# Gated linear attention with an ELU layer on one core: states of both halves in the first small group, values two slots later in one group with the next sums of logarithms, seam transfers on the sync queue

## The chip, the cores and the metric

The kernel runs on one core of a Trainium2 chip. The metric is the device time in microseconds of one execution. The engines are named as in the profile: PE is TensorE's matmul side and PEld its weight load, DVE is VectorE, ACT is ScalarE, POOL is GpSimd, SP is SyncE, which here only issues DMAs. Each engine takes its instructions in the order in which they stand in its queue; between engines, semaphores order what depends on each other.

## The reference

Two parts. The first is a gated recurrence over 768 positions, for 4 sequences and 8 heads of dimension 48, with a complex decay per position, head and row. The second is a two-layer network with an ELU over the 3072 x 384 outputs of the first (weights 384 x 2048 and 2048 x 384).

```python
mag = np.sqrt(a_re * a_re + a_im * a_im)
scale = np.minimum(mag, 0.999) / (mag + 1e-06)
...
for t in range(S):
    ar, ai = (a_re_n[:, :, t, :, None], a_im_n[:, :, t, :, None])
    new_re = ar * S_re - ai * S_im
    new_im = ar * S_im + ai * S_re
    kv = np.einsum('bhd,bhe->bhde', k[:, :, t], v[:, :, t])
    S_re, S_im = (new_re + kv, new_im)
    y[:, :, t] = np.einsum('bhd,bhde->bhe', q[:, :, t], S_re)
...
h = x @ w_in
g = np.where(h > 0.0, h, np.exp(np.minimum(h, 0.0)) - 1.0)
return g @ w_out
```

All data are float32 (the weights come as float64 and are rounded on the chip).

## The kernel before

The work is cut into twelve groups `u` = 0 to 11 (`NU`), each of two sequences (`NB`, here called the two halves `n`) times 128 positions (`C`), and each half into two chunks of 64 positions (`L`, index `c`). Groups 4 and up (`PAIRED`) are all done in the same way, and the change concerns these.

For one group the recurrence goes as follows. The decays become logarithms and angles: `squares` (L709, L710 on ACT), `joined` (L716 on POOL), `logarithms` (L735, L736), `powers` (L746, L747), `lengths` (L772 on DVE; its result is `l`), `ratios` (L759, L760 on POOL), `slopes` (L780 on DVE), `angles` (L815 on ACT) and `carried` (L821 on DVE). `decays` sums the logarithms along the positions: `quartered` makes four matmuls of 64x64 weights and 384 columns (L883) into two `w` buffers, and six exponentials on ACT (L893) turn them into the scales `E` and `F`; a DMA on ACT's queue stores the last rows of `E`, from which `ends` fetches the chunk decays `T`. `turns` sums the angles (L832 on PE), `waves` takes sine and cosine, `scaled` and `gated` apply them to the keys and queries, `transposed` (L1008) turns those.

Then come the small groups of matmuls. `scored` makes the products of keys and values of the first half (`state_products(u, 0)`, L1048, two `w` buffers), the scores of both halves (L1118, into the buffer `y`), the new states of the first half (`state_sums`: L1063 on DVE adds, L1065 on POOL multiplies with `T`) and the masked scores (L1125 on DVE). `valued` makes the products of the second half (L1048), the scores times the values of both halves (`value_products`, L1081), the states of the second half (L1063, L1065), the old states times the queries (`carried_products`, L1090, sorted by chunk), and copies the result to `x` and `y` in SBUF (L1144, L1145 on ACT). `seam` moves the rows of the last pairs of heads from `y` to their places in `x`: six DMAs of 16 KB (L1157), issued by POOL from group 2 on.

The layer of a group follows its attention: eight times `inner` (twelve recorded matmuls of 256 columns each, L1177, into a `mlp` buffer) with `elu` (L1186 and L1187 on ACT, L1188 on DVE), and `folded` (L1261 on DVE). The second product is made as seven products `k` on combined blocks, each in two parts `h` of four matmuls (eight records of 192 columns, L1283), in the order (1,0), (4,0), (1,1), (4,1), (6,0), (6,1), (5,0), (5,1), (7,0), (7,1), (2,0), (2,1), (3,0), (3,1). Products 1, 2 and 6 share one `mlp` buffer, one PSUM bank: 1 and 2 fill its first half of columns, 6 its second. After (1,1) ACT copies the first half to SBUF (L1291), and after (6,1) DVE adds the second half to that copy (L1295). Results go out through `o` buffers (L1302 on ACT, L1304 on DVE) by DMAs of the sync queue (L1305).

The order of all this is a table written by hand. `put(at, fn, ...)` gives each step a slot, the steps are sorted by slot, and each engine gets its instructions in that order (no scheduler changes it). A group has 16 slots; with `r = (u - 2) * 16`, the layer of group `u - 1` is multiplied out in slots r + 28 to r + 36 while group `u` is in `valued` and group `u + 1` is prepared. In these slots stood, in order: product (1,0), `logarithms` and `powers` of the next group (r + 28), (4,0), (1,1), `valued` and `seam` (r + 29.3), `lengths` and `ratios` of the next, (4,1), (6,0), (6,1), `slopes`, `decays` of the next (r + 31), (5,0) and so on; `turns` of the next at r + 34; the `inner` steps that read `x` begin at r + 36. `test_fetch` (L665, L670) loads pieces of the weights on the sync queue for a check by DVE (L680).

PSUM has three `w` buffers, three `mlp` buffers and one `y` of two banks.

Of the kernel before, what the change touches and what calls it, by code (L numbers as in the profile page):

```python
# [16 lines left out]
C = 128  # L17
# [488 lines left out]
def kernel(  # L506
# [13 lines left out]
    B, H, S, D = q.shape  # L520
    DM, DF = moe_w_in.shape[0], moe_w_out.shape[0]
    NI, NF = DM // C, DF // C
# [48 lines left out]
    def work(shape, tag="w"):  # L571
        return ps.tile(shape, FP32, tag=tag, bufs=3, name=tag)
# [120 lines left out]
    def new(tag, bufs=1, shape=None):  # L693
        return sb.tile(shape or [C, NB, H, D], FP32, tag=tag, bufs=bufs, name=tag)
# [182 lines left out]
    def quartered(u):  # L877

        x = nat[u]
        both = [work([C, HD]) for n in range(NB)]  # L880
        for c in range(C // L):
            for n, t in enumerate(both):
                nc.tensor.matmul(  # L883
                    t[ts(c ^ n, L)], lhsT=sum_logs[ts(c, L), ts(c, L)],
                    rhs=flat(x["l"][ts(c, L), n : n + 1]), start=True, stop=True,
                )
        for n, t in enumerate(both):
            for key, sign in (("E", 1.0), ("F", -1.0)):
                pairs = [(slice(0, C), slice(0, C))]
                if n:  # L890
                    pairs = [(ts(c, L), ts(1 - c, L)) for c in range(C // L)]
                for to, of in pairs:
                    nc.scalar.activation(  # L893
                        out=flat(x[key][to, n : n + 1]), in_=t[of], func=AF.Exp, scale=sign
                    )
        ends = dram.tile([NB, C // L, H, D], FP32, tag="ends", bufs=2, name="ends")
        nc.scalar.dma_start(
            out=ends.rearrange("n c h d -> c n (h d)"),
            in_=x["E"][L - 1 :: L].rearrange("p n h d -> p n (h d)"),
        )  # L900
        x["ends"] = ends
# [11 lines left out]
    def decays(u):  # L913
        x = nat[u]
        if u > 1:
            x["E"], x["F"] = new("n", 6), new("n", 6)
            quartered(u)
            return
        for n in range(NB):
            x["sums", n] = work([C, HD])  # L920
            nc.tensor.matmul(
                x["sums", n], lhsT=sum_logs, rhs=x["l"][:, n].rearrange("p h d -> p (h d)"),
                start=True, stop=True,
            )
            decayed(u, n)
# [103 lines left out]
    def state_products(u, n):  # L1029

        x = nat[u]
        b, s = where(u)
        x["S", n] = [state.get(b + n)]
        if s == S - C:
            last = C // L - 1
        else:
            last = C // L
        x["G", n] = gs = [
            work([C, H, D], "w" if u else "mlp") for c in range(last)
        ]  # L1040
        for h in range(H):
            for c, g in enumerate(gs):
                k = gates["k"][ts(c, L), n, h]
                parts = [(g[ts(i, HP), h], k[:, i]) for i in range(2)]
                if u == 0:
                    parts = [(g[:, h], k.rearrange("p i d -> p (i d)"))]
                for to, of in parts:
                    nc.tensor.matmul(  # L1048
                        to, lhsT=of, rhs=vn[u % 2][ts(c, L), n, ts(h, D)], start=True, stop=True,
                    )  # L1050

    def state_sums(u, n, chunks=range(C // L)):
        x = nat[u]
        for c, g in list(enumerate(x["G", n])):
            if c not in chunks:
                continue
            old = x["S", n][-1]
            new_s = new("S", 8, [C, H, D])
            wide = x["T"][:, n, c].unsqueeze(2).to_broadcast([C, H, D])
            if old is None:  # L1060
                nc.vector.tensor_tensor(out=new_s, in0=g, in1=wide, op=ALU.mult)
            else:
                nc.vector.tensor_tensor(out=new_s, in0=g, in1=old, op=ALU.add)  # L1063
                eng = nc.vector if u < 2 else nc.gpsimd
                eng.tensor_tensor(out=new_s, in0=new_s, in1=wide, op=ALU.mult)  # L1065
            x["S", n].append(new_s)
        state[where(u)[0] + n] = x["S", n][-1]
# [17 lines left out]
            )  # L1085
    def carried_products(u, n, y):
        x = nat[u]
        for p, c, j in EACH if u < PAIRED else sorted(EACH, key=lambda x: x[1]):
            if x["S", n][c] is not None:
                nc.tensor.matmul(  # L1090
                    y[ds(j * HP, D), c, ts(p, L)], lhsT=x["S", n][c][:, 2 * p + j],
                    rhs=x["qt", n][:, 2 * p + j, ts(c, L)], start=False, stop=False,
                    skip_group_check=True,
                )
# [15 lines left out]
    def scored(u):  # L1110

        x = nat[u]
        state_products(u, 0)
        t = ps.tile([C, NB, 512], FP32, tag="y", bufs=1, name="y")
        for n in range(NB):
            for h in range(H):
                for c in range(C // L):
                    nc.tensor.matmul(  # L1118
                        t[ts(c, L), n, ts(h, L)], lhsT=x["kt", n][:, h, ts(c, L)],
                        rhs=x["qt", n][:, h, ts(c, L)], start=True, stop=True,  # L1120
                    )
        for n in range(NB):
            state_sums(u, 0, [n])
            x["a", n] = new("a", 2, [C, H, L])
            nc.vector.tensor_tensor(  # L1125
                out=x["a", n], in0=t[:, n].rearrange("p (h t) -> p h t", h=H),
                in1=mask.unsqueeze(1).to_broadcast([C, H, L]), op=ALU.mult,
            )

    def valued(u):  # L1130

        x = nat[u]
        y = ps.tile([C, C // L, 512], FP32, tag="y", bufs=1, name="y")
        state_products(u, 1)
        for n in range(NB):
            value_products(u, n, y[:, :, ts(n, NP * L)], n == 0)
        state_sums(u, 1)
        for n in range(NB):
            carried_products(u, n, y[:, :, ts(n, NP * L)])
        x["x"], x["y"] = new("x", 2, [C, NI, GT]), new("y", 1, [C, GT])  # L1140
        parts = y.rearrange("p c (n x t) -> p c n x t", n=NB, x=NP)
        to = x["x"].rearrange("p x (n c t) -> p c n x t", n=NB, c=C // L)
        for c in range(C // L):
            nc.scalar.copy(out=to[:, c], in_=parts[:, c, :, 0:NI])  # L1144
        nc.scalar.copy(  # L1145
            out=x["y"].rearrange("p (n c t) -> p c n t", n=NB, c=C // L), in_=parts[:, :, :, NI],
        )

    def seam(u):

        x = nat[u]
        for j in range(2):
            for i in range(NI):
                eng = nc.scalar if u < 2 and j else nc.gpsimd
                if u == 0 and i == NI - 1:
                    eng = nc.sync
                eng.dma_start(  # L1157
                    out=x["x"][ds(j * HP + D, G), i], in_=x["y"][ds(j * HP + i * G, G)]
                )
# [232 lines left out]
    def put(at, fn, *args):  # L1392
        if fn is hidden:
            plan.append((at, len(plan), inner, args))
            plan.append((at, len(plan), elu, args))
        else:
            plan.append((at, len(plan), fn, args))
# [8 lines left out]

    def gates_of(u, *at):
        for x, fn in zip(at, (decays, turns, waves, scaled, ends, gated)):
            put(x, fn, u)

    def values_of(u, *at):
        fns = (transposed, "q"), (transposed, "k"), (scores,), (states,), (values,)
# [77 lines left out]
    for u in range(2, NU):  # L1490
        r = (u - 2) * SLOTS
        put(r + 8, load_a, u)
        put(r + 8, load_v, u)
        put(r + 8, load_qk, u)
        if u == 2:
            decays_of(u, 16, 17, 17, 18.4, 19.5, 19.6, 22.7, 19.8, 19.8)
            gates_of(u, 20.4, 21.6, 22.1, 22.4, 22.4, 22.6)
        else:
            decays_of(u, r + 11, r + 12, r + 12, r + 13.4, r + 13.5, r + 14.9, r + 16.7, r + 15.5, r + 16.6)
            gates_of(u, r + 15, r + 18, r + 18.5, r + 18, r + 18, r + 19.5)  # L1500
        if u < PAIRED:
            values_of(u, *(max(r + 22, 24.5) + x for x in (0, 1, 2, 3, 5, 4, 5, 6, 7, 8, 9)))
        else:
            for n in range(NB):
                put(r + 22 + 2 * n, transposed, u, "q", n)
                put(r + 23 + 2.3 * n, transposed, u, "k", n)
            put(r + 26.6, scored, u)
            put(r + 29.3, valued, u)
            put(r + 29.3, seam, u)
        layer_of(u, range(r + 36, r + 44), range(r + 44, r + 52))  # L1510
    for m in range(NR):
        put(40 + 4 * m, test_fetch, m)
# [42 lines left out]
```

## Time and profile before

| What | Value |
|---|---|
| Median of three runs | 698.71 us (697.7 to 698.75) |
| Profiled execution, whole | 700.76 us |
| Its span, first to last instruction | 699.0 us |
| Mean granted TensorE clock | 0.991 |
| Groups 4 to 11: start of `scored` (first L1048) | 249.00, 302.27, 355.70, 408.97, 462.25, 515.51, 570.23, 624.95 us |
| L1065 on POOL, mean | 936 ns |
| L1048 on PE, 1280 records of 64x64 | 25.8 us busy |
| L1157 on POOL's queue, 65 issues | 31.9 us busy, landing after 1.6 us (median) |

The profile's lines name engine, source line, operation and tiles; a float32 matmul leaves two records. In the timeline the columns are start, length, engine, line, operation, tiles, and the number of instructions merged; a bracket holds the idle time ahead and what ended it. Matmuls are pipelined and their ends are modelled, so lengths on PE are best read as the distance from one start to the next. A list of waits gives the total, the number of times and the longest.

### The profile page before, as it was taken

To read this page: it belongs to the slowest core of one execution; us is meant where nothing else is said; L and a number is where in the kernel's file an instruction comes from. 1 tells how busy PE (TensorE), PEld (TensorE's weight loads), DVE (VectorE), ACT (ScalarE), POOL (GpSimd) and SP (SyncE) were. 2 spreads that over 40 slices of the span, in tenths; PEclk is the share of its full clock that TensorE was granted. 3 is DMA by queue.
4 is the path that set the end of the run, shared out by engine and by line. 5 is a ranking of instruction groups with operands and counts; after the bars stand their busy time and mean duration, and the time that the engine had idled before them with its cause. 6 is when DMAs were issued, how large, how long until landed. Compare 5 with 4: busy or idle time off the path is not lost.

```text
span 699.0 us, 15744 instructions
## 1 busy us (share of the span) xinstructions
PE 665.2 (95%) x6656; PEld 580.0 (83%) x6656; DVE 399.6 (57%) x579; ACT 397.5 (57%) x622; POOL 201.6 (29%) x207
## 2 busy tenths in 40 slices
PE   8899899998999999999999999999999999999996
PEld 6777786565788898898998998998998888889995
DVE  5889999814857554555555555555555644742151
ACT  6875445658556754755755655656656547551230
POOL 2000000125423425425425415415408305402000
PEclk9899999999999999999999999999999999999999
DMA  9995746062082902911911821931831731200000
GB/s 163 174 160 94 156 150 173 10 115 53 3 137 67 144 26 63 141 31 59 142 37 53 131 52 53 131 55 51 118 67 30 143 63 31 69 1 8 23 1 28
DMA packets 149899, 55.98 MB, mean 80 GB/s; under 512 B 129172, under 2 KB 142652, under 8 KB 149820
## 3 DMA queue, kind: packets, MB, share of 16 engines
q1 hardware_dynamic: 146240, 53.53, 40.7%
q0 software_dynamic: 3360, 1.22, 1.3%
q8 instruction: 54, 0.88, 0.6%
q14 instruction: 25, 0.20, 0.1%
q10 hardware_dynamic: 220, 0.14, 0.1%
HBM read 48.88 MB, written 4.78 MB: 77 GB/s over the span
## 4 chain that ended last, share of the span: by engine, by line
PE 72%; DVE 11%; ACT 7%; POOL 5%; issue 3%; DMA 1%; ACTq 1%; POOLq 0%; DVEq 0%
PE mlp L1177 32%; PE mlp L1283 19%; PE w L1008 6%; DVE g L1261 3%; PE y L1118 2%; PE w L1048 2%; PE mlp L1198 2%; PE w L832 2%; PE y L1090 2%; DVE n L780 1%; DVE g L1188 1%; POOL S L1065 1%; PE w L1016 1%; DVE wf L43 1%; PE mlp L1386 1%
## 5 line engine op out<-in xcount | busy, mean ns | idle before, releaser
L1177 PE MATMUL mlp<-x,w_in 128*128 128x256 f32 x1152 | 262.3, 382 | 2.9 <-DVE g L1188 2.4
L1177 PEld LDWEIGHTS mlp<-x,w_in 128*128 128x128 f32 x1152 | 215.8, 191 | 32.5 <-DVE g L1188 2.8
L1188 DVE SCALAR_TENSOR_TENSOR g<-ee,mlp 128x512 f32<-128x512 f32 x96 | 65.5, 685 | 125.4 <-ACT ee L1187 119.2
L1186 ACT ACTIVATE ee<-mlp 128x512 f32<-128x512 f32 x96 | 57.3, 597 | 133.6 <-PE mlp L1177 125.4
L1283 PE MATMUL mlp<-w_out,g 128*128 128x192 f32 x640 | 110.3, 326 | 0.0
L1283 PEld LDWEIGHTS mlp<-w_out,g 128*128 128x128 f32 x640 | 105.4, 190 | 2.7
L1065 POOL TENSOR_TENSOR S<-S,T 128x384 f32<-128x384 f32 x36 | 33.7, 936 | 192.0 <-DVE S L1063 192.0
L1261 DVE TENSOR_TENSOR g<-g 128x512 f32<-128x512 f32 x80 | 67.3, 842 | 2.7
L1187 ACT ACTIVATE ee<-ee 128x512 f32<-128x512 f32 x96 | 60.5, 631 | 2.9
L1283 PEld LDWEIGHTS mlp<-w,g 128*128 128x128 f32 x320 | 52.0, 190 | 5.1 <-issue 4.8
L1283 PE MATMUL mlp<-w,g 128*128 128x192 f32 x320 | 56.0, 329 | 0.0
L856 POOL DMA_DIRECT2D carry<-n x10 | 5.3, 525 | 137.4 <-DVE n L840 137.4
L988 POOL TENSOR_TENSOR kg<-k,cs 128x1536 f32<-128x1536 f32 x9 | 38.6, 4294 | 19.8 <-issue 19.7
L1157 POOL DMA_DIRECT2D x<-y x65 | 31.9, 497 | 43.2 <-ACT y L1105 37.1
L893 ACT ACTIVATE n<-w 64x384 f32<-64x384 f32 (+1 forms) x60 | 28.1, 486 | 27.8 <-PE w L883 27.1
L1302 ACT COPY o<-mlp 128x192 f32<-128x192 f32 x10 | 3.2, 319 | 63.7 <-DMA out_dram<-o 52.9
L780 DVE SCALAR_TENSOR_TENSOR n<-n 128x768 f32<-128x768 f32 x11 | 13.7, 1247 | 35.7 <-POOL n L760 35.7
L1198 PE MATMUL mlp<-w_out,g 128*128 128x384 f32 x96 | 32.9, 490 | 0.7 <-DVE g L1188 0.7
L1063 DVE TENSOR_TENSOR S<-w,S 128x384 f32<-128x384 f32 x38 | 21.0, 553 | 21.5 <-PE w L1048 11.7
L1009 ACT COPY qt<-w 128x512 f32<-128x512 f32 x48 | 25.6, 581 | 12.7 <-PE w L1008 12.7
L716 POOL TENSOR_TENSOR n<-n 128x768 f32<-128x768 f32 x9 | 19.8, 2197 | 40.1 <-ACT n L710 40.1
L1090 PE MATMUL y<-qt,S 128*48 128x64 f32 x704 | 25.0, 222 | 6.0 <-POOL S L1065 4.1
(173 smaller groups left out, 988.5 us busy)
## 6 DMA issues: line engine op xcount, KB each, us to landing
w<-in_moe_w_out_dram SPq DMA_DIRECT2D x8, 768.0 KB
g<-in_moe_w_in_dram SPq DMA_DIRECT2D x16, 384.0 KB
g<-in_moe_w_out_dram SPq DMA_DIRECT2D x16, 384.0 KB
w<-in_moe_w_in_dram SPq DMA_DIRECT2D x16, 288.0 KB
vn<-in_v_dram SPq DMA_DIRECT2D x24, 192.0 KB
out_dram<-o SPq DMA_DIRECT2D x48, 96.0 KB
ar<-in_a_re_dram SPq DMA_DIRECT2D x22, 192.0 KB
ai<-in_a_im_dram SPq DMA_DIRECT2D x22, 192.0 KB
```

What stands on the lines that cost most here:

```text
L988: eng.tensor_tensor(out=to[:, :, :, 0:D], in0=each.unsqueeze(2).to_broadcast([C, step * H, 2, D]), in1=x["cs"][:, n * H : (n + step) * H], ...
L1008: nc.tensor.transpose(t[:, h], of, ident)
L1065: eng.tensor_tensor(out=new_s, in0=new_s, in1=wide, op=ALU.mult)
L1090: nc.tensor.matmul(y[ds(j * HP, D), c, ts(p, L)], lhsT=x["S", n][c][:, 2 * p + j], rhs=x["qt", n][:, 2 * p + j, ts(c, L)], start=False, st ...
L1157: eng.dma_start(out=x["x"][ds(j * HP + D, G), i], in_=x["y"][ds(j * HP + i * G, G)])
L1177: nc.tensor.matmul(t[:, e], lhsT=w_in[:, i, ts(f + e, C)], rhs=x["x"][:, i], start=(i == 0), stop=(i == NI - 1),)
L1186: nc.scalar.activation(out=e, in_=t, func=AF.Relu, scale=-1.0)
L1187: nc.scalar.activation(out=e, in_=e, func=AF.Exp, scale=-1.0)
L1188: nc.vector.scalar_tensor_tensor(out=x["g", f // 8][:, f % 8 : f % 8 + 2], in0=e, scalar=-1.0, in1=t, op0=ALU.add, op1=ALU.max)
L1198: nc.tensor.matmul(x["o", n], lhsT=x["g", f // 8][:, f % 8, ts(n, C)], rhs=w_out[:, f], start=(f == 0), stop=(f == NF - 1),)
L1261: nc.vector.tensor_tensor(out=S_of(u, k, h), in0=a, in1=b, op=op)
L1283: nc.tensor.matmul(to, lhsT=a[:, m], rhs=b[:, m], start=(first and h == 0 and m == 0), stop=False, skip_group_check=True,)
```

## The change

Three edits for the groups from 4 on, of which the second has two sides.

1. `scored` makes the products and the new states of both halves; of the four product buffers three are `w` and the last is a `mlp` buffer. `valued` makes none. `carried_products` is no longer sorted by chunk.
2. `valued` and `seam` of groups 4 to 10 stand at r + 31 in place of r + 29.3, so behind product (6,1) and not behind (1,1). The separate `decays` of groups 5 to 11 goes away: its matmuls (`quartered`) stand in `valued` of the group before, between `value_products` and `carried_products`, and its exponentials (`quarters_used`, with the DMA of `ends`) stand ahead of the copies to `x` and `y`. Group 11 keeps its slot.
3. `seam` is issued on the sync queue.

```diff
 def quartered(u):
...
+        return both
+
+    def quarters_used(u, both):
+        x = nat[u]
         for n, t in enumerate(both):
             for key, sign in (("E", 1.0), ("F", -1.0)):
...
         x["G", n] = gs = [
-            work([C, H, D], "w" if u else "mlp") for c in range(last)
+            work([C, H, D], "w" if u and not (u >= PAIRED and c and n) else "mlp")
+            for c in range(last)
         ]
...
-        for p, c, j in EACH if u < PAIRED else sorted(EACH, key=lambda x: x[1]):
+        for p, c, j in EACH:
...
     def scored(u):
-        state_products(u, 0)
+        for n in range(NB):
+            state_products(u, n)
...
         for n in range(NB):
-            state_sums(u, 0, [n])
+            for c in range(NB):
+                state_sums(u, c, [n])
...
     def valued(u):
-        state_products(u, 1)
         for n in range(NB):
             value_products(u, n, y[:, :, ts(n, NP * L)], n == 0)
-        state_sums(u, 1)
+        if u + 1 < NU:
+            both = quartered(u + 1)
         for n in range(NB):
             carried_products(u, n, y[:, :, ts(n, NP * L)])
+        if u + 1 < NU:
+            z = nat[u + 1]
+            z["E"], z["F"] = new("n", 6), new("n", 6)
+            quarters_used(u + 1, both)
...
-                if u == 0 and i == NI - 1:
+                if u >= PAIRED or u == 0 and i == NI - 1:
                     eng = nc.sync
...
         for x, fn in zip(at, (decays, turns, waves, scaled, ends, gated)):
-            put(x, fn, u)
+            if fn is not decays or u <= PAIRED:
+                put(x, fn, u)
...
-            put(r + 29.3, valued, u)
-            put(r + 29.3, seam, u)
+            put(r + (31 if u + 1 < NU else 29.3), valued, u)
+            put(r + (31 if u + 1 < NU else 29.3), seam, u)
```

More of the change, by code (lines that the diff above doesn't have):

```diff
@@ L916, in decays @@
             x["E"], x["F"] = new("n", 6), new("n", 6)
-            quartered(u)
+            quarters_used(u, quartered(u))
             return
```

## The prediction

> **What bounds the kernel now.** I read the busy shares first, then the chain that ended last, then who waited for whom from 240 us on (where groups 4 to 11 run), then the timeline of one group.
>
> ```profile
> PE 665.2 (95%) x6656; PEld 580.0 (83%) x6656; DVE 399.6 (57%) x579; ACT 397.5 (57%) x622; POOL 201.6 (29%) x207
> ...
> PE 72%; DVE 11%; ACT 7%; POOL 5%; issue 3%; DMA 1%; ACTq 1%; POOLq 0%; DVEq 0%
> ```
>
> TensorE (PE) is the bound; the others have slack on average. So a microsecond that PE stands still from group 4 on is one on the end. Of PE's own idle time after 240 us two kinds are large:
>
> ```profile
> PE y L1090 <- POOL S L1065: 4.1, 5, 0.9
> PE w L832 <- DVE n L821: 2.4, 2, 1.2
> ```
>
> The timeline of the window around group 9's `valued` shows the first kind, and beside it what ScalarE (ACT) does at that time:
>
> ```profile
> 521.30 1.46 PE L1283 MATMUL mlp<-w_out,g 128*128 128x192 f32 x8
> 522.60 1.46 PE L1283 MATMUL mlp<-wt,g 128*128 128x192 f32 x8
> 522.66 0.83 ACT L709 ACTIVATE n<-ar 128x768 f32<-128x768 f32 x1
> 523.90 1.46 PE L1283 MATMUL mlp<-w_out,g 128*128 128x192 f32 x8
> 525.29 1.15 PE L1048 MATMUL w<-vn,kg 64*64 64x48 f32 x64
> 526.26 1.13 PE L1081 MATMUL y<-a,vn 64*64 64x64 f32 x64
> 527.32 1.21 PE L1090 MATMUL y<-qt,S 128*48 128x64 f32 x34
> 529.64 0.83 ACT L747 ACTIVATE n<-n 128x768 f32<-128x768 f32 x1
> 529.77 0.65 PE L1090 MATMUL y<-qt,S 128*48 128x64 f32 x16 [0.43 <-POOL S L1065]
> 530.36 1.57 PE L1283 MATMUL mlp<-wt,g 128*128 128x192 f32 x8
> 530.37 0.30 ACT L1291 COPY ee<-mlp 128x192 f32<-128x192 f32 x1
> 531.76 2.76 PE L1283 MATMUL mlp<-w,g 128*128 128x192 f32 x16
> 534.46 0.88 PE L883 MATMUL w<-n,sum_logs 64*64 64x384 f32 x8
> ```
>
> Three products (1,0), (4,0), (1,1) of the layer, 1.30 us each, then `valued` (L1048, L1081, L1090), then (4,1) at 530.36, (6,0) and (6,1) from 531.76, then `decays` (L883). Note L1291: ScalarE's copy of product 1 out of PSUM. Product 1 is done at 525.2, but the copy runs only at 530.37, because ScalarE takes its work in order, and squares, table loads, logarithms and exponentials of the next group (L709 to L747) stand ahead of it.
>
> **What the skill says.** (1) The Trainium skill, "TensorE: Matmul & The Clock Gate", Part 1 ("What's actually happening"): PE falls to half clock after an idle window of about 3.4 us, and comes back after a busy one; the windows run freely. The trace agrees, and adds that a window need not be wholly idle:
>
> ```profile
> 47.00:48.00 1.00, 0.72 (x16) 1.00 1.08 189
> 48.00:49.00 1.00, 1.00 (x5) 0.80 1.14 193
> 49.00:50.00 1.00, 1.00 (x4) 0.50 0.98 236
> ```
>
> (columns: stretch, its length, PE busy, granted clock, DMA share, GB/s). From 48.6 to 52.0 the clock is 0.50, one stretch of 3.4 us, after 2 us of matmuls of two columns (L935); twelve L1177 matmuls there take 4.38 us to the next start in place of 2.60. (2) "PSUM — Partial Sum Buffer", "PSUM bank collisions raise a hardware error": two engines may not touch one bank in the same partitions at once, even at other columns, so a dependency is put between them. In the trace of before no such wait shows. (3) "TensorEngine Tiling (Array Packing)", "Key Properties": a change of tiling mode drains PE. The trace agrees: 525.29 less 523.90 is 1.39 where a product takes 1.30, so 0.09 us.
>
> **The change part by part.** I count from P, the start of (1,0) (521.30 here). Seven windows have the moved `valued` (groups 4 to 10; group 11's stays).
>
> States early. 64 records of L1048 (0.97 us) leave `valued` for `scored`: nothing on PE. Their waits are covered: the third `w` buffer is freed by ScalarE's copies of the keys a product earlier, the `mlp` buffer by VectorE long before. VectorE's two extra sums (0.55 each) lie in the 2.3 us it waits for ScalarE before L1188. What goes: the wait of L1090 for GpSimd's L1065. From the start of L1090 to the next start the seven windows take 3.05, 3.20, 3.05, 3.04, 3.04, 3.04, 3.04; group 11, which had its state ready, 1.92. The gain is 21.46 - 13.44 = 8.0 us.
>
> One group fewer. Around L883: 0.09 to enter, 0.80 itself, 0.10 more than 2.60 for the sixteen records after it: 0.99. Inside a 64x64 group it costs 0.65 (its four positions lie side by side, two 384-column passes at twice a 192-column record's 0.163) to 0.80. Gain 0.19 to 0.34, I take 0.27: 1.9 us in seven.
>
> Seam on the sync queue. Six issues of 0.49 leave GpSimd (2.93 us a group), and group 0's two on SP cost 0.59 each, so 3.5 us there. Behind them stand a test fetch and four output stores; ahead of them a fetch that went at P + 7.1. ScalarE now does six exponentials (2.9 us) before the copies of x (1.25), so x lies ready 2.9 + 1.25 + 3.5 + 1.6 (landing) = 9.3 us after L883; its reader L1177 starts 1.92 + 8 x 1.30 + 1.45 = 13.8 after it. Cost nothing; without that cover, up to 6 us a group if landing took some 10 us.
>
> GpSimd loses the seam and two L1065 ahead of the ratios L759, which then start at 529.64 + 0.83 = 530.5 in place of 534.95. So L780 and L821 come over 3 us earlier, and ScalarE's 1.25 us of copies ahead of the angles are paid by the 1.92 us of L1090 that now follow L883 on PE. The 1.21 us wait of L832, twice, goes: gain 2.4 us.
>
> `valued` two slots later. This is the step that decides. Product 6 writes the other half of the PSUM bank whose first half L1291 copies, and in the built program of both kernels (6,0)'s first matmul waits for the count on ScalarE's semaphore that just this copy raises. Before, five microseconds of `valued` stood between (1,1) and (4,1), so PE came to (6,0) at P + 10.46, after the copy's end at P + 9.37 (530.67 - 521.30; 9.38 in groups 4 and 7). Now `valued` comes after (6,1): PE does (1,0), (4,0), (1,1), (4,1) and is at (6,0) at P + 5.20. ScalarE's work ahead of the copy is unchanged and hangs on the layer's last inner product, which ends at P; only 0.26 us of it is idle. So PE stands from 5.20 to 9.37 + 0.05: 4.22 us, seven times 29.5 us. All that is queued on PE stands with it: (6,1), `valued`, L883. Nothing else of PE's order is there to fill it. L883's own need, L772, can start at P + 8.5 and ends by P + 9.5, hidden in it.
>
> The clock after that stall. An idle 4.22 us splits at worst into 2.1 and 2.1 over two free windows of 3.41: one window is then at least 62% idle. The trace bounds the trigger from both sides: 1.67 us idle in one window (75.90 to 79.32) left the clock at 1.00; about 2.2 us of next to no work (45.2 to 48.6) dropped it. So I expect a window at half clock after nearly every stall, 3.41 / 2 = 1.7 us of lost work; 0.7 to 1.3 if the window ends within the stall, up to 3.0 if PE takes a second window to come back, as it did from 21.3 to 28.1. Bounds: 0 to 21 us in all; I take 7 x 1.7 = 12.
>
> Sum against the profiled execution, 700.76 us (span 699.0 and 1.8 around it): 700.8 - 8.0 - 1.9 - 2.4 + 29.5 + 12 = 730. The shown runs' median, 698.71, lies 2.05 lower, so 727.9: I say 728.
>
> **Rivals.**
> (a) The same stall, but the clock holds: 698.71 + 17.2 = 716. For it: the page speaks of a whole idle window, which 4.22 us holds only in a quarter of positions. Against: the drop at 48.6 without one.
> (b) PE isn't held at (6,0), and the kernel is faster. Its place is L1291: the copy would have to end early. It decides at P + 6.96: then the stall of 1.76 eats just the 8.0 + 1.9 + 2.4 = 12.3 us that are gained. If it ends before P + 5.2, PE reaches L883 at P + 8.95 while L772 ends at P + 9.5, a new wait of some 0.5 us, 3.5 in all; 698.7 - 12.3 + 3.5 = 690. For it: in the last layer, with no next group, the copy does follow (1,1) at once, and there is no wait. Against: ScalarE's order, the same in both kernels there, puts L1291 behind L747.
> (c) Worse: two windows at half clock after most stalls, 7 x 3.0: 737. For it: 21.3 to 28.1. Against: there 1.7 us of idleness lay within the second window; here PE is busy after the stall.
>
> **How the numbers follow.** Forecast (722 to 733) 0.64, (a) 713 to 722: 0.23, (b) 0.09, (c) 0.04. Leaving out (b) and (c) gives 713 to 733. A measurement of this kernel tells some 0.2% from no change; of (b) I give 0.01 to a time within that. Slower by more: 0.91.
>
> **What would show it.** Right: PE idle about 4.2 us ahead of product 6 in seven windows, ended by ScalarE's copy; half clock right after; no idle time before L1090 and L832; L883 directly between the two parts of `valued`; `x` landing well before its L1177. Wrong: the copy standing right behind (1,1) on ScalarE; a clock of 1.00 throughout (then 716); or PE waiting for `x`, L772 or the states instead.

## The result, and the profile after

The changed kernel takes 731.01 us (median of four runs, 729.57 to 733.4) against 698.73 before (also four): the ratio is 1.047 (95% interval 1.044 to 1.050). Its profiled execution, the slowest of the four, took 733.4 us, with a span of 731.7 and a mean granted clock of 0.966 (0.991 before). Absolute times of the same kernel differ by up to 0.3% between occasions (the kernel before had medians of 698.7 to 700.7), so the experiments below are compared by their ratios to the kernel before.

The page of the changed kernel, part 1, then two of its costliest groups (line, engine, operation, tiles, count, then busy time and mean, then the idle time ahead and what ended it):

```profile
PE 677.1 (93%) x6656; PEld 593.2 (81%) x6656; DVE 395.9 (54%) x579; ACT 398.5 (54%) x622; POOL 176.0 (24%) x159
...
L1295 PE MATMUL mlp<-w_out,g 128*128 128x192 f32 x640 | 110.3, 326 | 0.0
...
L1295 PE MATMUL mlp<-w,g 128*128 128x192 f32 x320 | 70.5, 384 | 28.4 <-ACT ee L1303 28.4
```

PE has the same 6656 instructions and a smaller share of a longer span. Both groups are the same matmuls, and the first is unchanged (326 ns). The second are products 6 and 5: 28.4 us of idle time ahead of them, ended by L1303, which is L1291 of before (ScalarE's copy of product 1), and 384 ns in place of 329. The same group before:

```profile
L1283 PE MATMUL mlp<-w,g 128*128 128x192 f32 x320 | 56.0, 329 | 0.0
```

The waits of PE after 240 us, the ones of before being gone:

```profile
PE mlp L1295 <- ACT ee L1303: 28.4, 7, 4.1
```

No wait of L1096 (L1090 before) for GpSimd and none of L832 for VectorE is left; there is one kind, seven times, at most 4.1 us. The timeline around group 9's `valued`, the same place as before:

```profile
548.41 1.46 PE L1295 MATMUL mlp<-w_out,g 128*128 128x192 f32 x8
...
549.71 1.46 PE L1295 MATMUL mlp<-wt,g 128*128 128x192 f32 x8
...
551.01 1.46 PE L1295 MATMUL mlp<-w_out,g 128*128 128x192 f32 x8
...
552.31 1.46 PE L1295 MATMUL mlp<-wt,g 128*128 128x192 f32 x8
...
556.74 0.83 ACT L747 ACTIVATE n<-n 128x768 f32<-128x768 f32 x1
...
557.47 0.30 ACT L1303 COPY ee<-mlp 128x192 f32<-128x192 f32 x1
...
557.82 4.54 PE L1295 MATMUL mlp<-w,g 128*128 128x192 f32 x16 [4.05 <-ACT ee L1303]
...
562.30 1.16 PE L1087 MATMUL y<-a,vn 64*64 64x64 f32 x64
...
563.28 0.83 PE L883 MATMUL w<-n,sum_logs 64*64 64x384 f32 x8
...
564.03 1.99 PE L1096 MATMUL y<-qt,S 128*48 128x64 f32 x64
...
565.96 2.87 PE L1295 MATMUL mlp<-w,g 128*128 128x192 f32 x16
```

P is 548.41. Products (1,0), (4,0), (1,1), (4,1) stand back to back and end at P + 5.20; the copy ends at 557.77, P + 9.36; (6,0) starts at P + 9.41. Then the sixteen records of product 6 take 4.48 us to the next start, and the same kind at 565.96 takes 2.70. The clock tells why (columns: stretch, length, busy time and count of PE, PEld, DVE, ACT and POOL in turn, granted clock, DMA share, GB/s):

```profile
554.00:556.00 2.00, 0.00 (x0) 0.00 (x0) 1.41 (x3) 1.97 (x3) 0.00 (x0) 1.00 0.00 0
...
558.00:560.00 2.00, 2.00 (x10) 2.00 (x11) 0.00 (x0) 0.00 (x0) 1.92 (x2) 0.71 0.00 2
560.00:562.00 2.00, 2.00 (x8) 1.86 (x6) 0.00 (x0) 0.00 (x0) 1.38 (x1) 0.50 0.00 0
562.00:564.00 2.00, 2.00 (x74) 1.14 (x72) 1.53 (x3) 0.00 (x0) 0.00 (x0) 0.94 0.00 0
```

PE stands while ScalarE is busy 1.97 of 2.00 us, and then works at half clock until 562.2, where the clock comes back.

### The profile page after: what moved, and what is told of

Read it like the earlier page. It is cut to its first block, busy times and chain, and to the rows that moved or that the text cites. A ratio compares the mean times of both kernels' runs of the same rounds, so it can differ in the third digit from the quotient of the medians.

```text
span 731.7 us, 15769 instructions
## 1 busy us (share of the span) xinstructions
PE 677.1 (93%) x6656; PEld 593.2 (81%) x6656; DVE 395.9 (54%) x579; ACT 398.5 (54%) x622; POOL 176.0 (24%) x159
## 4 chain that ended last, share of the span: by engine, by line
PE 73%; issue 6%; ACT 5%; DVE 5%; POOL 5%; SPq 3%; DMA 2%; ACTq 0%; POOLq 0%; DVEq 0%
PE mlp L1189 28%; PE mlp L1295 22%; PE w L1013 5%; PE mlp L1210 4%; PE y L1096 3%; PE w L1054 2%; POOL n L716 2%; SPq L596 2%; PE y L1125 2%; PE y L1087 2%; PE w L832 2%; POOL S L1071 1%; PE w L1210 1%; ACT n L746 1%; ACT n L736 1%
## 5 line engine op out<-in xcount | busy, mean ns | idle before, releaser
L1189 PE MATMUL mlp<-x,w_in 128*128 128x256 f32 x1152 | 260.6, 381 | 2.6 <-DVE g L1200 2.6
L1189 PEld LDWEIGHTS mlp<-x,w_in 128*128 128x128 f32 x1152 | 214.6, 190 | 31.9 <-DVE g L1200 3.0
L1295 PE MATMUL mlp<-w,g 128*128 128x192 f32 x320 | 70.5, 384 | 28.4 <-ACT ee L1303 28.4
L1295 PEld LDWEIGHTS mlp<-w,g 128*128 128x128 f32 x320 | 64.3, 227 | 31.9 <-ACT ee L1303 30.5
L1071 POOL TENSOR_TENSOR S<-S,T 128x384 f32<-128x384 f32 x36 | 29.3, 830 | 168.4 <-DVE S L1069 168.4
L993 POOL TENSOR_TENSOR kg<-k,cs 128x1536 f32<-128x1536 f32 x9 | 41.0, 4551 | 20.1 <-issue 20.0
L821 DVE SCALAR_TENSOR_TENSOR n<-carry,n 1x768 f32<-1x768 f32 x10 | 9.5, 946 | 45.3 <-ACT n L815 45.3
L1295 PE MATMUL mlp<-wt,g 128*128 128x192 f32 x160 | 29.2, 327 | 0.0
L993 DVE TENSOR_TENSOR qg<-q,cs 128x1536 f32<-128x1536 f32 (+1 forms) x12 | 19.5, 1623 | 17.4 <-ACT cs L971 17.4
L1013 PE MATMUL w<-ident,kg 128*128 128x128 f32 x192 | 26.0, 280 | 2.3 <-POOL kg L993 1.4
```

The lines of the kernel that those rows point to most:

```text
L993: eng.tensor_tensor(out=to[:, :, :, 0:D], in0=each.unsqueeze(2).to_broadcast([C, step * H, 2, D]), in1=x["cs"][:, n * H : (n + step) * H], ...
L1013: nc.tensor.transpose(t[:, h], of, ident)
L1189: nc.tensor.matmul(t[:, e], lhsT=w_in[:, i, ts(f + e, C)], rhs=x["x"][:, i], start=(i == 0), stop=(i == NI - 1),)
L1295: nc.tensor.matmul(to, lhsT=a[:, m], rhs=b[:, m], start=(first and h == 0 and m == 0), stop=False, skip_group_check=True,)
```

## The experiments

**The bank.** Is it the copy that holds product 6, and the shared bank that makes it do so? Product 6 gets its own buffer:

```diff
-            1: (0, 0, True), 2: (0, 0, False), 6: (0, 1, False), 5: (1, 0, True),
+            1: (0, 0, True), 2: (0, 0, False), 6: (3, 1, True), 5: (1, 0, True),
...
-            x["p", bank] = work([C, 2, HN], "mlp")
+            x["p", bank] = work([C, 2, HN], "w" if bank == 3 else "mlp")
```

> The changed kernel, but product 6 fills a PSUM buffer of its own (a w buffer) instead of the second half of the bank that ScalarE copies. My theory: PE no longer waits at product (6,0) for that copy, so the 4.22 us stalls (29.5 us in seven groups) and the half clock after them (15.1 us by the distances from (6,0) to (5,0)) both go; L883 then meets the result of L772 about 0.5 us early, a new wait of some 3.5 us in all: 731.0 - 29.5 - 15.1 + 3.5 = 690 us (686 to 694). Rival: the stall belongs to the place of valued itself (ScalarE's or VectorE's later work is needed by product 6 anyway, for instance the folded blocks of L1273): then 725 to 731.

Measured: ratio 0.988 (0.984 to 0.993), which is 690.6 us on the scale of 698.7. PE's timeline around group 9's `valued`, with the own bank:

```profile
523.36 1.46 PE L1295 MATMUL mlp<-wt,g 128*128 128x192 f32 x8
524.66 2.76 PE L1295 MATMUL w<-w,g 128*128 128x192 f32 x16
527.36 1.16 PE L1087 MATMUL y<-a,vn 64*64 64x64 f32 x64
528.94 0.88 PE L883 MATMUL w<-n,sum_logs 64*64 64x384 f32 x8 [0.42 <-DVE n L772]
```

Product 6 follows (4,1) after 1.30 us, at full clock, and the wait that comes next is the one for L772, 0.42 us where 0.5 was expected. This one buffer turns the change from 4.7% slower to 1.2% faster. The rival, that product 6 needs the late work anyway, falls. A buffer of its own is here also a bank of its own, so this run doesn't tell whether the wait is kept by the buffer or by the bank.

**ScalarE's order.** The other way to take the hold away: leave the bank and make the copy early, with the next group's logarithms and powers behind (1,1):

```diff
-            decays_of(u, r + 11, r + 12, r + 12, r + 13.4, ...
+            decays_of(u, r + 11, r + 13.2, r + 13.2, r + 13.4, ...
```

> The changed kernel with the next group's logarithms and powers put behind product (1,1), so that ScalarE makes its copy of product 1 ahead of them; banks and all else as in the changed kernel. My theory: the copy is done at about P + 4.3, PE is not held at (6,0), and the logarithms come some 1.1 us later, so that L883 waits for L772 about 1.6 us in place of 0.4: 698.7 - 8.0 - 2.4 - 2.4 + 7 x 1.6 = 697 us, ratio 0.997; up to 1.013 if so short a stop drops the clock as well. Rival: the order on ScalarE is not what holds product 6: 731.

Measured: ratio 0.9986 (0.9973 to 1.0000). The waits of PE in this kernel are one kind:

```profile
PE w L883 <- DVE n L772: 10.8, 7, 1.6
```

1.6 us a group at L883, as expected, and the clock stays at 1.00 after them. So both halves of the explanation are shown: the shared buffer and the order on ScalarE. Moving the copy forward takes the loss away but gains next to nothing over the kernel before, because the logarithms that had to make room are what PE needs next.

**The clock.** Idle matmuls fill the stall, without letting PE go further:

```diff
+    def fill(n):
+
+        t = work([C, C])
+        for _ in range(n):
+            nc.tensor.matmul(t, lhsT=ident, rhs=ident, start=True, stop=True)
...
             put(r + 26.6, scored, u)
+            if u + 1 < NU:
+                put(r + 30, fill, 17)
```

> The changed kernel with 17 idle matmuls (identity by identity, 128 columns, into a spare w buffer) ahead of product (6,0) in each of the seven groups, some 3.7 us of them: they lie where PE stands anyway. My theory: PE still comes no further than the copy, but the clock stays at 1.00, so 731.0 - 15.1 = 716 us (714 to 719). Rival: the distance of 8.1 to 9.4 us after the stall has another cause than the clock: 731 or, with the fillers in the way, more.

Measured: ratio 1.029 (1.027 to 1.031), 719 us on the scale of 698.7. PE around group 9's `valued` with 17 fillers (L1405):

```profile
543.68 3.96 PE L1405 MATMUL w<-ident 128*128 128x128 f32 x34
547.90 2.87 PE L1295 MATMUL mlp<-w,g 128*128 128x192 f32 x16 [0.26 <-ACT ee L1303]
550.70 1.16 PE L1087 MATMUL y<-a,vn 64*64 64x64 f32 x64
```

Product 6 begins at the same distance from (4,1), 547.90 - 542.38 = 5.52 us, but takes 2.80 in place of 4.48; from 240 us to the last matmul no stretch shows a clock below 1.00. Work that computes nothing saves some 12 us. It falls 3 us short of what was expected, and most of that is visible: in three groups the scores (L1125) stop for 0.6 to 1.0 us, which the changed kernel doesn't do. The filler's `w` buffer shifts the rotation there; that this is the reason was not tried.

With 9 fillers, 2.04 to 2.05 us stay idle in each of the seven groups.

> The changed kernel with 9 idle matmuls in place of 17 ahead of product (6,0), so that some 2.2 us of the stall stay idle. My theory: the clock drops when one free window of 3.4 us holds more than about 1.9 us of idleness (1.67 and 1.6 left it, 2.06 once dropped it), which 2.2 us do in about half of the positions: drops in three or four of seven groups, 1.033 to 1.043 of the time before. Rival: the clock falls only after about 3.4 us without work: no drop, 1.029 as with 17.

Measured: ratio 1.041 (1.037 to 1.045). The number lies inside the expectation, but not for its reason: in the profiled execution the clock fell in all seven groups, not in half. Two of them (columns: stretch, length, PE busy, clock, DMA share, GB/s):

```profile
441.00:442.00 1.00, 1.00 (x6) 0.67 0.06 16
442.00:443.00 1.00, 1.00 (x5) 0.50 0.00 0
```
```profile
267.00:270.00 3.00, 3.00 (x12) 0.54 0.00 1
270.00:273.00 3.00, 3.00 (x85) 0.89 0.00 0
```

From these shares the drops begin at 441.34 and 267.24, 174.1 us apart, which is 51 windows of 3.413. The fillers end near 438.6 and 264.5, so the idle 2.05 us lie whole within one window both times. The groups of this kernel follow each other after about 58.0 us, 17 windows, so all seven meet the same position: within this execution the draw of positions that I counted on didn't take place. For the other three (728.18, 732.56 and 726.45 us, mean clock 0.979, 0.970 and 0.984, against 731.61 and 0.973 here) it isn't shown. The rival, that only some 3.4 us without work would do it, falls.

**States alone.** Edit 1 on the kernel before, except that `carried_products` stays sorted by chunk:

```diff
-            work([C, H, D], "w" if u else "mlp") for c in range(last)
+            work([C, H, D], "w" if u and not (u >= PAIRED and c and n) else "mlp")
+            for c in range(last)
...
     def scored(u):
...
-        state_products(u, 0)
+        for n in range(NB):
+            state_products(u, n)
...
-            state_sums(u, 0, [n])
+            for c in range(NB):
+                state_sums(u, c, [n])
...
     def valued(u):
...
-        state_products(u, 1)
...
-        state_sums(u, 1)
```

> The kernel before with the first edit alone: states of both halves in scored, everything else as it was. My theory: the waits of L1090 go (8.0 us), but valued is 2.1 us shorter then, so PE comes to (6,0) at P + 8.36, before ScalarE's copy ends at P + 9.37, and waits 1.0 us there; and GpSimd's seam still holds the ratios, so the angles come as late after P as before while PE comes to turns 1 us earlier, and waits at L832 in every group (0.7 us, 2 in the last two). All that is saved is given back: 700 to 705 us. Rival: a plain gain of the wait that was seen, 691 us.

Measured: ratio 1.014 (1.008 to 1.019), 708 us on the scale of 698.7, slower than I said. Its waits, and its wait at L832 in the window of group 9's `valued`:

```profile
PE w L832 <- DVE n L821: 6.5, 7, 2.1
PE mlp L1284 <- ACT ee L1292: 5.9, 7, 0.9
```
```profile
548.23 2.19 PE L832 MATMUL w<-n,sum_turns 128*128 128x384 f32 x4 [2.06 <-DVE n L821]
```

Both new waits are there, near the sizes expected (0.85 us at product 6; 0.47 at L832 in five groups and 2.06 in two). What I left out is the clock: after this 2.06 us it stood at 0.50 from 549.0 to 552.4, which costs at most 1.7 us, half of that stretch. The rest of the difference is not assigned. Removing the wait that the profile of before shows best, by itself, makes the kernel slower.

**Seam alone, and seam undone.** The one-line edit of the queue, on the kernel before, and taken back in the changed kernel:

```diff
-                if u == 0 and i == NI - 1:
+                if u >= PAIRED or u == 0 and i == NI - 1:
```

> The kernel before with the third edit alone, the seam's DMAs on the sync queue. My theory: GpSimd comes to the ratios 3 us earlier, the waits of L832 in the last two groups (2.4 us) go, nothing else on PE changes: ratio 0.9966 (696.3 us). Rival: nothing or a loss, because six DMAs of 0.59 us stand ahead of fetches and stores on the sync queue: 1.000 or above.

> The changed kernel with the seam's DMAs issued by GpSimd again. My theory: the seam's queue costs nothing and saves nothing in the changed kernel, since PE stands for the copy and comes to turns late enough: 731 us within 2. Rival: the transfers on the sync queue hold up x, stores or fetches and are part of the loss: below 728.

Measured: alone 0.9954 (0.9938 to 0.9969), with no wait of L832 left; undone in the changed kernel 1.048 (1.043 to 1.053) against 1.047. The same edit is worth half a per cent where PE comes to L832 ahead of the angles, and nothing that could be measured where PE is held up before.

What made the two waits of L832 in the kernel before can be read more closely than the prediction did. GpSimd's seam stood ahead of the ratios in all seven windows, but PE waited only in those of groups 9 and 10. There L780 was slow:

```profile
538.69 2.55 DVE L780 SCALAR_TENSOR_TENSOR n<-n 128x768 f32<-128x768 f32 x1 [3.70 <-POOL n L760]
```

In the five other windows it took 0.96 us. In these two, a GpSimd instruction of 1.81 us (L976) had started 0.07 to 0.08 us ahead of L780. In the states-alone kernel the same two windows show the same pair, and their waits exceed the other five by 1.59 us (2.06 against 0.47), just what L780 takes longer. With the seam alone L780 starts about 3 us earlier, before L976, and takes 0.96 us in all seven. So, as these traces read, the late start that the seam causes was needed, but the 1.2 us come from this overlap; no run changes L780 or L976 alone.

**A version that beats both.** First, valued and decays unmoved: states early, seam on the sync queue, product 6 in its own buffer (the diffs above, on the kernel before).

> The kernel before with states of both halves in scored, the seam on the sync queue, and product 6 in a buffer of its own; valued and decays stay where they were. My theory: no wait is left at (6,0), L1090 or L832, so 698.7 - 8.0 - 2.4 = 688 us, ratio 0.985: moving valued and joining the groups is worth only the 2.4 us of the joined group. Rival: without the move something else waits (L832 for the angles, x for its landing): above 0.99.

Measured: 0.985 (0.983 to 0.988). After 240 us no wait of PE for another engine is left, only stops of 0.2 to 0.6 us of its weight loads where the form of the matmuls changes. Then the moved and joined groups with the own bank, and the sums of logarithms later, so that L772 is in time: behind all of L1096, or between its halves. The second of these, against the changed kernel:

```diff
-        if u + 1 < NU:
-            both = quartered(u + 1)
         for n in range(NB):
             carried_products(u, n, y[:, :, ts(n, NP * L)])
+            if u + 1 < NU and n == 0:
+                both = quartered(u + 1)
```

> The changed kernel with product 6 in a buffer of its own, and the sums of logarithms behind L1096 in place of ahead of it. My theory: PE comes to L883 1.9 us later, when L772 is long done, so the 0.42 us waits of the own-bank kernel go (2.9 us in seven), less up to 0.2 us a group for one more change of tiling: ratio about 0.985 (688 us). Rival: the changes of tiling cost as much as the wait: 0.988 as before.

> The changed kernel with product 6 in a buffer of its own, and the sums of logarithms between the two halves of L1096. My theory: PE comes to L883 1 us later, after L772, and ScalarE's angles still come before PE is at L832 (1.9 us later made L832 wait 0.57 us, so the slack is some 1.2 us): neither wait is left, two more changes of tiling cost up to 0.2 us a group: ratio 0.984 to 0.988 (688 to 690 us), as good as the kernel with valued unmoved. Rival: L832 waits in every group again: 0.990.

Measured: behind, 0.991 (0.989 to 0.994), a miss; between, 0.986 (0.983 to 0.989). The miss has its line in the waits of the kernel with the sums behind:

```profile
PE w L832 <- DVE n L821: 4.0, 7, 0.6
```

L883 1.9 us later makes the exponentials later, behind which ScalarE makes the angles, and PE waits at L832 0.57 us in every group. Between the halves neither wait is left. The best joined version and the unmoved one can't be told apart by their ratios (0.986 and 0.985), and their traces agree: from the start of `scored` of group 4 to that of group 11 it is 364.99 us joined and 365.06 unmoved (375.95 before). With product 6 in its own buffer, the move and the join together are worth nothing that could be measured here.

## Why the prediction was right

It said 728 us (713 to 733); measured are 731.0. Step by step, with the sizes that the changed kernel's profile shows (of its slowest execution, so the clock's share is that of this one):

- The hold at product 6, said 4.22 us and 29.5 in all: from the start of (4,1) to the start of (6,0) it is 5.51 or 5.52 in all seven groups, less 1.30: 29.5. Shown to be the shared buffer (own bank) and ScalarE's order (copy first).
- The clock, said 12, bounds 0 to 21: from the start of (6,0) to the start of (5,0) the seven groups take 9.43, 8.85, 8.14, 8.08, 8.86, 8.14, 8.07; with 17 fillers, at full clock, 6.46. The excess is 59.57 - 45.22 = 14.4 us. In four groups it is 1.6 to 1.7 us, the 1.7 that was said. In three (9.43, 8.85, 8.86) it is 2.4 to 3.0: there the half clock began while PE still stood (at 265.3, 323.3 and 497.4). For that case the prediction expected the least, 0.7 to 1.3, and its argument against rival (c) was that PE is busy after the stall. But the first window at half clock held the end of the stall itself, and a second one followed. Rival (c) expected two such windows after most stalls; they came after three of seven. So the term was sized rightly for four groups and too small for three. Rival (a), a clock that holds, fell in seven of seven.
- States early, said 8.0: from the start of L1096 it is 1.92 or 1.93 to the next start everywhere, so 8.0 is right as a term. By itself it is given back (states alone).
- One group fewer, said 1.9: with L883 inside, L1087 to L1096 takes 0.98 + 0.75 = 1.73; in group 11, without it, 1.09. So it costs 0.64 there in place of 0.99, 2.4 in all.
- The wait of L832, said 2.4: gone. The seam alone takes it away too, so moving the seam off GpSimd's queue is what removes it; that L780 was slowed beside L976 in just these two windows, the prediction didn't say.
- Cover for the seam: its issues run from 568.22 for 3.68 us and land 1.8 after, so by 573.7; L1189 reads `x` at 577.75. Nothing waited, and the seam undone changes nothing that could be measured.

The sum, 29.5 + 14.4 - 8.0 - 2.4 - 2.4 = 31.1 us, stands against 32.6 between the two profiled executions. Of the rest 0.7 lies ahead of group 4 (its `scored` starts at 249.74 in place of 249.00), in code that the change leaves alone. Some 0.8 us are not assigned.

The decisive step can't be read from the profile of before as a wait, since there the copy's lateness was hidden by `valued` itself: what was moved was the cover of another wait. It was found by asking of each step behind the moved one what it waits for, and when that is done.

## What to carry to other kernels

When a block of work moves on the engine that bounds, list the waits of what now comes earlier, hidden ones too, and compare each releaser's end with the new time of arrival: a block that looks like a cost may be the cover of a late copy on an in-order engine. A PSUM buffer (here one bank) that two products share was a dependency even between halves that never meet; another buffer for one product was worth some 40 us here. And price a stall on TensorE twice when it is long enough: once for itself, once for the half clock after it. Here every stall of 4.1 us and all seven of 2.05 us dropped the clock, one of two of 2.06 us did, and those of 1.6 us did not.

## What the runs showed of the hardware that I had not expected

The granted clock falls on much less than an idle window. In the states-alone kernel two waits of 2.06 us stood in like surroundings. One lay whole within a window (546.17 to 548.23; the drop at 549.0 marks the window's end), and the clock fell; the other (603.43 to 605.50) was cut by the window's edge near 603.6 into 0.2 and 1.9 us, and it held. The kernel with the seam undone narrows it further. One of its stalls ended at about 497.1, and the drop that followed at 498.45 puts the edges of the two windows before it at 495.04 and 491.63 (columns: stretch, length, PE busy, clock, DMA share, GB/s):

```profile
491.63:495.04 3.41, 1.42 (x9) 1.00 0.00 0
495.04:498.45 3.41, 1.34 (x8) 1.00 0.38 120
```

The first window, with 1.99 us idle, left the clock at 1.00; the second, with 2.07, dropped it. With 9 fillers 2.04 us were enough. So in these kernels, from 240 us on, the trigger lies between 1.99 and 2.04 us of idleness in a window of 3.41, by the profile's busy times. The Trainium skill, "TensorE: Matmul & The Clock Gate", Part 1, names an idle window as what brings the half clock; the measurements here differ from it, and they decide. That page's freely running windows agree with the 51 whole windows above.

And a window that begins idle doesn't bring the clock back: after the stall that ended at 499.31 the clock stayed at 0.50 from about 497.4 to 504.2, two windows, though PE worked the last 1.5 us of the first without a break. After the stall that ended at 265.88 even 2.81 us of work in the window from 265.28 to 268.69 didn't do it. Work at half clock counted by half, 2.81 us are 1.4 us, about the 1.34 to 1.42 at which a window at full clock fell or held. That both are one limit, on the work done in a window, is a guess from these few windows and was not tested.
